# Polysketch attention and a channel block: key features, kv and numerators in 64-column tiles, key products on GpSimd, and a reordered first chunk

## The chip, the cores and the metric

The kernel runs on one core of one Trainium2 chip. The metric is the device time of one execution in microseconds, the median of several runs. The profile is of one execution; its span starts with the first profiled instruction and ends with the last, so it is some microseconds shorter than the time.

The engines are named as in the profile: PE is TensorE (PEld its weight loads), DVE is VectorE, ACT is ScalarE, POOL is GpSimd, SP is SyncE, which here only issues DMAs.

## The reference

Attention with a polynomial sketch in place of the softmax, and then a normalised channel block with a residual. There are 4 batches, 4 heads, 1088 tokens and a head width of 32; the sketch has r = 8, so a feature vector has 64 elements.

```python
def phi(x):                                   # S1, S2: 8 x 32
    a = np.einsum('rd,bhsd->bhsr', S1, x)
    b = np.einsum('rd,bhsd->bhsr', S2, x)
    return np.einsum('bhsi,bhsj->bhsij', a, b).reshape(*x.shape[:-1], 64)
q_p, k_p = phi(q), phi(k)
kv  = np.einsum('bhsf,bhsd->bhfd', k_p, v)
z   = np.sum(k_p, axis=2)
num = np.einsum('bhsf,bhfd->bhsd', q_p, kv)
den = np.einsum('bhsf,bhf->bhs', q_p, z)[..., None] + 1e-06
x   = (num / den) -> (4, 1088, 128)           # heads side by side
# channel block
xn  = (x - mean) / sqrt(var + 1e-06) * g_ln   # over the 128 channels
out = x + np.maximum(xn @ w_ch1, 0.0) @ w_ch2 # w_ch1 128 x 512, w_ch2 512 x 128
```

`S1`, `S2`, `g_ln`, `w_ch1` and `w_ch2` arrive as float64. [...]the kernel rounds them to float32 from their bit patterns.

## The kernel before

Everything is float32. The tokens are taken in 9 chunks: two chunks of 512 tokens for each batch (chunks 0 to 7), and the last 64 tokens of all four batches together as chunk 8. A float32 product of matrices is two passes in the profile, each with its weight load, so a line that issues one `matmul` shows two MATMUL records.

The pieces that the change touches. The features of the keys, in three parts of a batch (512, 512 and 64 tokens): a product into PSUM (`kf`), a copy to SBUF (`fs`), and the outer product of the two sketches (`kp`) on VectorE. The copy of v into a tile with a column of ones for each head is on GpSimd.

```python
def key_features(b, part):
    ...
    nc.gpsimd.tensor_copy(out=<v1, heads 33 apart>, in_=<vn>)
    kf = ps.tile([P, 512], F32, tag="xk", name="kf", bufs=1)      # shared with xp
    for i in range(tiles):
        nc.tensor.matmul(kf[0:m, 64*i : 64*i+64], kT[:, P*i : P*i+m], sk, ...)
    nc.scalar.copy(fs[0:m, 0:64*tiles], kf[0:m, 0:64*tiles])
    nc.vector.tensor_tensor(out=<kp>, in0=<fs, a repeated>, in1=<fs, b repeated>, op=ALU.mult)
```

The sum over the keys, `kv` and `z` in one product (33 columns a head). Two heads go in one product of 128 x 66, of which only the two diagonal blocks are used:

```python
def key_values(b):
    for t in range(NT):                       # 9 tiles of tokens
        for pair in range(2):
            nc.tensor.matmul(kvp[:, c], kp[0:m, <2 heads, 128 columns>], v1[0:m, <66 columns>], ...)
    for i in range(2):
        nc.vector.tensor_copy(out=<kvz, diagonal block>, in_=<kvp, diagonal block>)
```

The queries: `ab` holds both sketches repeated (64 rows, 128 columns), `qb` is a copy of one of them on ScalarE, `qp` their product on VectorE. The numerators `nd` (and denominators) are products with 128 tokens as columns; in the last chunk, where four batches share a tile, with 32:

```python
def numerators(c, i2):
    for i in range(2):
        for pair in range(2):
            if c < LAST:
                nc.tensor.matmul(nd[:, o:o+66], qp[:, <128 tokens>], kvzs[b][:, pc], ...)
            else:
                for b in range(B):
                    nc.tensor.matmul(nd[32*b : 32*b+32, o:o+66], qp[:, t:t+32], kvzs[b][:, pc], ...)
    den = nd + 1e-6; rden = 1/den; x = nd * rden     # VectorE
```

The channel block of a chunk: `x` is transposed (`xp`, then the copy `xT` on ScalarE), four products with the first weight (`hp`, then `hT` with the ReLU on ScalarE), sixteen with the second (`po`), and the sum `ob` on VectorE. Centring is folded into the first weight (`w1p`), and the inverse root of the variance is applied only in `ob`. The variance is `bn_stats` and `bn_aggr` on VectorE, a square root on ScalarE, and five small VectorE operations (`root`).

The order of work, which fixes the order in each engine's queue (`nb` is the next batch, in every even chunk):

```python
for c in range(LAST + 1):
    nb = ...
    if nb: key_rows(nb, 0); key_rows(nb, 1)
    hidden(c, 0); hidden(c, 1)
    query_features(c + 2, 0)
    hidden(c, 2)
    if nb: key_features(nb, 0)
    hidden(c, 3)
    numerators(c + 1, 0); numerators(c + 1, 1)
    if nb: key_rows(nb, 2); key_features(nb, 1)
    statistics(c + 1)
    second(c)
    if nb: key_features(nb, 2)
    root(c + 1)
    result(c)
    turn_x(c + 1)
    query_rows(c + 3)
    query_features(c + 2, 1)
    if nb: key_values(nb)
```

Ahead of the loop stand the rounding of the weights, the keys of batch 0, and the queries and numerators of chunk 0. The rounding of a weight is three bit operations on VectorE, five arithmetic operations on GpSimd, one more on VectorE and a last product on GpSimd.

Of the kernel before, what the change touches and what calls it, by code (L numbers as in the profile page):

```python
# [23 lines left out]
def kernel(  # L24
# [27 lines left out]

    nc = tc.nc
# [7 lines left out]
    NT = 9  # L61
# [11 lines left out]
    ps = ctx.enter_context(tc.tile_pool(name="ps", bufs=2, space=bass.MemoryType.PSUM))  # L73
    ctx.enter_context(tc.manual_schedule())

# [4 lines left out]
    s_raw = raw_tile([R2, D], S1, "s_raw")  # L80
    nc.scalar.dma_start(out=s_raw[0:R, :], in_=S1)
    nc.sync.dma_start(out=s_raw[R:R2, :], in_=S2)

    kn, qn, vn = {}, {}, {}

    def load_rows(store, src, tag, b):
        t = store[b] = consts.tile([P, G * D], F32, name=f"{tag}{b}")
        nc.sync.dma_start(
            out=t, in_=bass.AP(src.tensor, src.offset + b * H * S * D, [[G * D, P], [1, G * D]])
        )  # L90

    def load_v(b):
        base = v.offset + b * H * S * D
        vt = vn[b] = consts.tile([P, NT * DM], F32, name=f"vn{b}")
        for p0 in range(4):
            nc.sync.dma_start(
                out=_ap(vt, 32 * p0, 32, 0, [[8 * D, H], [1, 8 * D]]),
                in_=bass.AP(
                    v.tensor, base + 8 * p0 * D, [[G * D, 32], [S * D, H], [1, 8 * D]]
                ),  # L100
            )
        for r in range(2):
            nc.sync.dma_start(
                out=_ap(vt, 32 * r, 32, 8 * DM, [[D, H], [1, D]]),
                in_=bass.AP(
                    v.tensor, base + (32 + r) * D, [[G * D, 32], [S * D, H], [1, D]]
                ),
            )

    load_rows(kn, k, "kn", 0)  # L110
    load_rows(qn, q, "qn", 0)
    g_raw = raw_tile([P, 1], moe_g_ln, "g_raw")
    nc.scalar.dma_start(out=g_raw, in_=moe_g_ln.rearrange("(p o) -> p o", o=1))
    w1_raw = raw_tile([P, DH], moe_w_ch1, "w1_raw")
    nc.scalar.dma_start(out=w1_raw, in_=moe_w_ch1)
    w2_raw = raw_tile([P, JC * DM], moe_w_ch2, "w2_raw")
    nc.scalar.dma_start(
# [3 lines left out]
    load_v(0)  # L121
    for b in range(1, B):
        load_rows(kn, k, "kn", b)
        load_v(b)
        load_rows(qn, q, "qn", b)


    def rounded(dst, raw, eng):

        np_, n = dst.shape
        words = raw.bitcast(U32)
        lo, hi = words[:, 0 : 2 * n : 2], words[:, 1 : 2 * n : 2]

        def temp(tag, dtype):
            return work.tile([P, n], dtype, tag=f"{tag}{n}", name=tag)[0:np_, :]

        bits, ex, sign = (temp(tag, U32) for tag in ("bits", "ex", "sign"))
        mant = temp("mant", F32)  # L140
        bit, two = nc.vector.tensor_scalar, nc.vector.scalar_tensor_tensor
        ts = eng.tensor_scalar
        bit(out=ex, in0=hi, scalar1=20, scalar2=0x7FF,  # L143
            op0=ALU.logical_shift_right, op1=ALU.bitwise_and)
        bit(out=bits, in0=hi, scalar1=0xFFFFF, scalar2=None, op0=ALU.bitwise_and)
        bit(out=sign, in0=hi, scalar1=0x80000000, scalar2=None, op0=ALU.bitwise_and)  # L146
        yield
        ts(out=ex, in0=ex, scalar1=1023.0 - 127.0, scalar2=0.0, op0=ALU.subtract, op1=ALU.max)
        ts(out=ex, in0=ex, scalar1=255.0, scalar2=None, op0=ALU.min)
        ts(out=mant, in0=bits, scalar1=2.0**-20, scalar2=1.0, op0=ALU.mult, op1=ALU.add)  # L150
        low = temp("low", F32)
        ts(out=low, in0=lo, scalar1=2.0**-52, scalar2=None, op0=ALU.mult)
        eng.tensor_tensor(out=mant, in0=mant, in1=low, op=ALU.add)
        yield
        two(out=ex, in0=ex, scalar=23, in1=sign, op0=ALU.logical_shift_left, op1=ALU.bitwise_or)
        eng.tensor_tensor(out=dst, in0=mant, in1=ex.bitcast(F32), op=ALU.mult)

    def as_f32(raw, name, eng):

        if raw.dtype == F32:  # L160
            return raw, iter(())
        t = consts.tile(list(raw.shape), F32, name=name)
        return t, rounded(t, raw, eng)


    warm = small.tile([P, 1], F32, tag="warm", name="warm")
    nc.vector.memset(warm, 1.0)
# [10 lines left out]
    for h in range(H):  # L178
# [3 lines left out]
    center = consts.tile([P, P], F32, name="center")  # L182
    nc.gpsimd.tensor_scalar(
        out=center, in0=ident, scalar1=-1.0 / DM, scalar2=None, op0=ALU.add
    )

    kvzs = [consts.tile([P, 2 * 2 * D1], F32, name=f"kvz{b}") for b in range(B)]
    v1s = [consts.tile([P, NT * W], F32, name=f"v1_{i}") for i in range(2)]
    for t in v1s:
        nc.gpsimd.memset(_ap(t, 0, P, D, [[D1, 8 * H]]), 1.0)  # L190
        nc.gpsimd.memset(_ap(t, 0, 64, 8 * W + D, [[D1, H]]), 1.0)
    for t in kvzs:
        nc.gpsimd.memset(t, 0.0)
# [13 lines left out]
    sp = ps.tile([P, 512], F32, tag="nd", name="sp")  # L207
# [7 lines left out]


    def blocks(dst, src, half):

        nc.vector.transpose(  # L219
            _ap(dst, 0, P, 0, [[32, 4], [P, 4], [1, 32]]),  # L220
            _ap(src, 0, P, 4 * half * D, [[8 * D, 4], [D, 4], [1, D]]),
        )
# [11 lines left out]
    def key_features(b, part):  # L234
        t0, tiles, m = (4 * part, 4, P) if part < 2 else (8, 1, 64)
        if part == 0:
            kps[b] = work.tile([P, NT * H * F], F32, tag="kp", name="kp")
        v1, kT, kp = v1s[b % 2], kTs.pop((b, part)), kps[b]
        vj = 8 if part < 2 else 1
        nc.gpsimd.tensor_copy(  # L240
            out=_ap(v1, 0, m, t0 * W, [[W, tiles], [D1, H], [1, D]]),
            in_=_ap(vn[b], 0, m, t0 * D if part < 2 else 8 * DM, [[D, tiles], [vj * D, H], [1, D]]),
        )
        kf = ps.tile([P, 512], F32, tag="xk", name="kf", bufs=1)
        for i in range(tiles):
            nc.tensor.matmul(  # L246
                kf[0:m, 64 * i : 64 * i + 64], kT[:, P * i : P * i + m], sk,
                start=True, stop=True,
            )
        fs = work.tile([P, 4 * H * R2], F32, tag="fs", name="fs")  # L250
        nc.scalar.copy(fs[0:m, 0 : 64 * tiles], kf[0:m, 0 : 64 * tiles])  # L251
        nc.vector.tensor_tensor(  # L252
# [6 lines left out]
    def key_values(b):  # L259
        kvp = ps.tile([P, 512], F32, tag="nd", name="kvp")  # L260
        v1, kp, kvz = v1s[b % 2], kps.pop(b), kvzs[b]

        for t in range(NT):
            m = P if t < 8 else 64
            for pair in range(2):
                c = slice(2 * D1 * pair, 2 * D1 * (pair + 1))
                nc.tensor.matmul(  # L267
                    kvp[:, c],
                    kp[0:m, H * F * t + 2 * F * pair : H * F * t + 2 * F * (pair + 1)],
                    v1[0:m, W * t + c.start : W * t + c.stop],  # L270
                    start=(t == 0 and pair == 0), stop=(t == NT - 1), skip_group_check=True,
                )
        for i in range(2):
            nc.vector.tensor_copy(  # L274
                out=_ap(kvz, F * i, F, D1 * i, [[2 * D1, 2], [1, D1]]),
                in_=_ap(kvp, F * i, F, D1 * i, [[2 * D1, 2], [1, D1]]),
            )

    qTs, qps, xs, rs, mvs, xTs, hTs, pos = {}, {}, {}, {}, {}, {}, {}, {}
# [14 lines left out]
    def query_features(c, i2):  # L294


        if c > LAST or (c == LAST and i2):
            return
        qT = qTs[c]
        ab = ps.tile([P, 1024], F32, tag="ab", name="ab", bufs=1)  # L300
        for o, w in ((0, wb), (256, wa)):
            for pair in range(2):
                rows = slice(64 * pair, 64 * pair + 64)
                nc.tensor.matmul(  # L304
                    ab[:, 512 * pair + o : 512 * pair + o + 256],
                    w[rows, :], qT[rows, 256 * i2 : 256 * i2 + 256], start=True, stop=True,
                )
        qb = work.tile([P, 512], F32, tag="qb", name="qb")
        two = [[256, 2], [1, 256]]
        nc.scalar.copy(_ap(qb, 0, P, 0, two), _ap(ab, 0, P, 0, [[512, 2], [1, 256]]))  # L310
        p = qps[c, i2] = work.tile([P, 512], F32, tag="qp", name="qp", bufs=4)
        nc.vector.tensor_tensor(  # L312
            out=_ap(p, 0, P, 0, two), in0=_ap(ab, 0, P, 256, [[512, 2], [1, 256]]),
            in1=_ap(qb, 0, P, 0, two), op=ALU.mult,
        )

    def numerators(c, i2):

        if c > LAST or (c == LAST and i2):
            return  # L320
        if i2 == 0:
            xs[c] = work.tile([P, 512], F32, tag="x", name="x", bufs=3)
        qp, x = qps.pop((c, i2)), xs[c]
        nd = ps.tile([P, 512], F32, tag="nd", name="nd")
        for i in range(2):
            for pair in range(2):
                o = W * i + 2 * D1 * pair
                pc = slice(2 * D1 * pair, 2 * D1 * (pair + 1))
                if c < LAST:
                    nc.tensor.matmul(  # L330
                        nd[:, o : o + 2 * D1],
                        qp[:, 256 * pair + P * i : 256 * pair + P * i + P],
# [210 lines left out]
```

## Time and profile before

| What | Value |
|---|---|
| time, median of 3 runs | 172.49 us (171.52 to 173.51) |
| span of the profiled execution | 168.6 us |
| PE busy, instructions | 141.2 us, 893 |
| PEld busy | 109.5 us |
| DVE busy, instructions | 88.6 us, 291 |
| ACT busy, instructions | 43.1 us, 86 |
| POOL busy, instructions | 26.9 us, 50 |
| HBM read, written | 7.74 MB, 2.23 MB |

In the groups of a profile, "L267 PE MATMUL kvp<-v,kp" is the matmul of line 267 that writes the tile kvp from v and kp; behind it stand the shape of the array's tile (rows*columns), the shape of the output and the number of records, and then the busy time, the mean duration of one in ns, and the idle time of the engine just ahead of it with what ended it. A mean duration of a matmul includes its way through the array; what a pass costs in a stream is the length of the stretch over the number of passes, as the chain gives it.

### The profile page before, as it was taken

Reading aid. Unit: us, or ns where it says so; the run is one execution under the profiler, and the core shown is the slowest. Engines: PE = TensorE matmul, PEld = TensorE weight load, DVE = VectorE, ACT = ScalarE, POOL = GpSimd, SP = SyncE. Lnnn points to the kernel's source line nnn. Section 1 sums busy time; section 2 is a strip of 40 time slices with the busy share of each in tenths; the row PEclk is TensorE's granted clock in tenths of the full one; section 3 lists DMA queues with packets and bytes.
Section 4 is the critical chain, followed back from the end, with each engine's and each line's share of the span. In section 5 each row is a group of like instructions: output and inputs, shape, how many; then the busy total and the mean of one; then the engine's idle time right before and its main releaser. Section 6 shows DMA issues by size and latency. Waiting matters only on the chain.

```text
span 168.6 us, 2403 instructions
## 1 busy us (share of the span) xinstructions
PE 141.2 (84%) x893; PEld 109.5 (65%) x893; DVE 88.6 (53%) x291; ACT 43.1 (26%) x86; POOL 26.9 (16%) x50
## 2 busy tenths in 40 slices
PE   0542999569079999999999999999999999989870
PEld 0441898544047978595697949759895884965760
DVE  4466102734954872178587326858761584662610
ACT  3010101014213030604512142362123316225130
POOL 7006940499440003000000000000000000000000
PEclk9999999999858999999999999999999999999999
DMA  4897899300000002001100200020020002002021
GB/s 122 292 219 235 259 288 303 118 4 2 0 0 0 0 0 68 0 0 40 26 0 0 62 4 0 9 57 0 4 62 0 0 4 62 0 8 54 4 62 33
DMA packets 7196, 10.13 MB, mean 60 GB/s; under 512 B 2320, under 2 KB 5008, under 8 KB 7184
## 3 DMA queue, kind: packets, MB, share of 16 engines
q1 hardware_dynamic: 6352, 8.92, 19.6%
q10 hardware_dynamic: 832, 1.05, 2.2%
q8 instruction: 7, 0.11, 0.3%
q14 instruction: 5, 0.04, 0.1%
HBM read 7.74 MB, written 2.23 MB: 59 GB/s over the span
## 4 chain that ended last, share of the span: by engine, by line
PE 83%; DVE 8%; DMA 3%; ACT 2%; issue 1%; SPq 0%; DVEq 0%; ACTq 0%
PE hp L406 19%; PE po L416 18%; PE ab L304 13%; PE kvp L267 12%; PE nd L330 9%; PE kf L246 6%; PE xp L397 3%; DMA kn<-in_k_dram 3%; DVE qT L219 1%; ACT fs L251 1%; DVE r L385 1%; DVE sign L146 1%; PE w1p L474 1%; DVE kp L252 1%; DVE ex L143 1%
## 5 line engine op out<-in xcount | busy, mean ns | idle before, releaser
L406 PE MATMUL hp<-xT,w 128*128 128x512 f32 (+1 forms) x72 | 35.4, 611 | 1.2 <-ACT xT L399 1.2
L416 PE MATMUL po<-w_f,hT 128*128 128x128 f32 x272 | 32.4, 277 | 0.0
L416 PEld LDWEIGHTS po<-w_f,hT 128*128 128x128 f32 x272 | 31.2, 192 | 0.1
L409 ACT ACTIVATE hT<-hp 128x512 f32<-128x512 f32 (+1 forms) x36 | 20.5, 573 | 27.1 <-PE hp L406 27.0
L312 DVE TENSOR_TENSOR qp<-ab,qb 128x512 f32<-128x512 f32 x17 | 11.6, 684 | 26.3 <-ACT qb L310 26.2
L304 PE MATMUL ab<-qT,wb 64*128 64x256 f32 x68 | 14.4, 493 | 10.6 <-DVE qT L219 10.6
L267 PEld LDWEIGHTS kvp<-v,kp 128*128 128x128 f32 (+1 forms) x144 | 20.3, 226 | 2.0 <-issue 1.0
L267 PE MATMUL kvp<-v,kp 128*128 128x66 f32 (+1 forms) x144 | 21.3, 314 | 0.0
L406 PEld LDWEIGHTS hp<-xT,w 128*128 128x128 f32 x72 | 12.0, 193 | 13.4 <-issue 6.4
L330 PEld LDWEIGHTS nd<-kvz,qp 128*128 128x128 f32 x128 | 17.1, 209 | 4.0 <-issue 4.0
L310 ACT COPY qb<-ab 128x512 f32<-128x512 f32 x17 | 10.0, 585 | 33.2 <-PE ab L304 33.2
L304 PEld LDWEIGHTS ab<-qT,wb 64*128 64x128 f32 x68 | 6.3, 214 | 18.1 <-issue 12.7
L252 DVE TENSOR_TENSOR kp<-fs 128x1024 f32<-128x1024 f32 (+1 forms) x12 | 11.8, 984 | 11.0 <-ACT fs L251 11.0
L330 PE MATMUL nd<-kvz,qp 128*128 128x66 f32 x128 | 16.9, 291 | 0.0
L246 PEld LDWEIGHTS kf<-sk,kT 128*128 128x128 f32 (+1 forms) x72 | 11.1, 227 | 7.4 <-issue 5.1
L246 PE MATMUL kf<-sk,kT 128*128 128x64 f32 (+1 forms) x72 | 12.0, 314 | 4.6 <-DVE kT L232 3.0
L304 PE MATMUL ab<-qT,wa 64*128 64x256 f32 x68 | 12.5, 436 | 0.0
L429 DVE SCALAR_TENSOR_TENSOR ob<-po,rstd,x 128x128 f32<-128x128 f32 x34 | 9.6, 344 | 4.4 <-PE po L416 4.3
L240 POOL COPY v<-vn 128x512 f32<-128x512 f32 (+1 forms) x12 | 5.8, 518 | 27.5 <-issue 16.4
L274 DVE COPY kvz<-kvp 64x66 f32<-64x66 f32 x8 | 1.8, 224 | 14.4 <-PE kvp L267 14.4
L372 ACT ACTIVATE r<-va 128x4 f32<-128x4 f32 (+1 forms) x9 | 1.8, 205 | 29.3 <-DVE va L369 29.3
L365 DVE BATCH_NORM_STATS2 st<-x 128x6 f32<-128x128 f32 x34 | 9.1, 266 | 0.0
(67 smaller groups left out, 105.6 us busy)
## 6 DMA issues: line engine op xcount, KB each, us to landing
kn<-in_k_dram SPq DMA_DIRECT2D x4, 544.0 KB, 4.8
qn<-in_q_dram SPq DMA_DIRECT2D x4, 544.0 KB, 5.5
vn<-in_v_dram SPq DMA_DIRECT2D x16, 128.0 KB, 5.5
out_dram<-ob SPq DMA_DIRECT2D x32, 64.0 KB, 1.7
w_raw<-in_moe_w_ch_dram ACTq DMA_DIRECT2D x2, 512.0 KB, 10.9
vn<-in_v_dram SPq DMA_DIRECT2D x8, 16.0 KB, 5.0
out_dram<-ob SPq DMA_DIRECT2D x4, 32.0 KB, 1.6
s_raw<-in_S_dram ACTq DMA_DIRECT2D x1, 2.0 KB
```

Of the source, the lines that this page charges most:

```text
L246: nc.tensor.matmul(kf[0:m, 64 * i : 64 * i + 64], kT[:, P * i : P * i + m], sk, start=True, stop=True,)
L252: nc.vector.tensor_tensor(out=_ap(kp, 0, m, t0 * H * F, [[F, tiles * H], [R, R], [1, R]]), in0=_ap(fs, 0, m, 0, [[R2, tiles * H], [1, R], ...
L267: nc.tensor.matmul(kvp[:, c], kp[0:m, H * F * t + 2 * F * pair : H * F * t + 2 * F * (pair + 1)], v1[0:m, W * t + c.start : W * t + c.stop ...
L304: nc.tensor.matmul(ab[:, 512 * pair + o : 512 * pair + o + 256], w[rows, :], qT[rows, 256 * i2 : 256 * i2 + 256], start=True, stop=True,)
L310: nc.scalar.copy(_ap(qb, 0, P, 0, two), _ap(ab, 0, P, 0, [[512, 2], [1, 256]]))
L312: nc.vector.tensor_tensor(out=_ap(p, 0, P, 0, two), in0=_ap(ab, 0, P, 256, [[512, 2], [1, 256]]), in1=_ap(qb, 0, P, 0, two), op=ALU.mult,)
L330: nc.tensor.matmul(nd[:, o : o + 2 * D1], qp[:, 256 * pair + P * i : 256 * pair + P * i + P], kvzs[CHUNKS[c][0]][:, pc], start=True, stop= ...
L365: nc.vector.bn_stats(out=st[:, 6 * i : 6 * i + 6], in_=x[:, DM * i : DM * (i + 1)])
L406: nc.tensor.matmul(hp[:, 0:n], w1[:, P * j : P * (j + 1)], xTs[c][:, 0:n], start=True, stop=True)
L409: nc.scalar.activation(hTs[c][:, 512 * j : 512 * j + n], hp[:, 0:n], AF.Relu)
L416: nc.tensor.matmul(po[:, DM * i : DM * (i + 1)], hT[:, 512 * j + P * i : 512 * j + P * i + P], w2[:, DM * j : DM * (j + 1)], start=(j == 0 ...
L429: nc.vector.scalar_tensor_tensor(out=ob[:, t], in0=po[:, t], scalar=rstd[:, i : i + 1], in1=x[:, t], op0=ALU.mult, op1=ALU.add,)
```

## The change

What it does, part by part:

- **64-column tiles.** `kf`, `kvp` and `nd` are computed in two tiles of 64 columns of the array, which alternate: key features and numerators take 64 tokens in each, and `kvp` one head in each, so that the unused off-diagonal blocks are no longer computed. The number of matmuls doubles.
- **Key outer products on GpSimd.** All but two of the parts (the first and third of batch 0). In exchange, the copies of kvz go from VectorE to ScalarE, and the copies of v for batch 0 to ScalarE.
- **The variance.** `bn_aggr` and the small operations of VectorE are replaced by ten small operations a chunk on GpSimd, which combine the two halves that `bn_stats` gives.
- **PSUM by hand.** One tile covers all eight banks, and each use names its bank: 0 and 1 for nd and half of ab, 2 and 3 for kf, kvp and the other half of ab, 4 and 5 for hp, 6 for po, 7 for xp.
- **The order.** The four products of `hidden` stand together; then the numerators of the next chunk, the keys or kv of the next batch, and `second`. Keys come in odd chunks, kv in even ones; both features of the queries of chunk c + 2 come last, between `xp` and the next `hidden`.
- **The head.** The first loads are split and reordered (the first 512 columns of k first, w1 before v). In the rounding, three steps go to ScalarE (ReLU and copy with bias and scale), and two of GpSimd's into VectorE operations. The gains go into `center` and no longer into w1.
- **Tokens.** A chunk has other tokens than before (16 consecutive ones for each group instead of 4 from each run of 8); loads and stores follow.

The diff, cut to its core:

```diff
-    ps = ctx.enter_context(tc.tile_pool(name="ps", bufs=2, space=bass.MemoryType.PSUM))
+    banks = ps.tile([P, 8 * 512], F32, name="banks")
...
 # loads
+    load_rows(kn, k, 0, 0, 512)
+    load_rows(kn, k, 0, 512)
+    nc.sync.dma_start(out=w1_raw, in_=moe_w_ch1)
+    load_v(0, 0)
+    load_rows(qn, q, 0, 0, 512)
+    load_v(0, 1)
+    load_v(0, 2)
+    load_rows(qn, q, 0, 512)
+    nc.sync.dma_start(out=w2_raw..., in_=moe_w_ch2...)
...
 # rounding
+        act(over, ex, AF.Relu, bias=low_e[0:np_, :])
+        act(ex, over, AF.Relu, bias=top_e[0:np_, :], scale=-1.0)
+        act(mant, bits, AF.Copy, bias=1.0, scale=2.0**-20)
         yield
+        stt(out=ex, in0=ex, scalar=23, in1=sign, op0=ALU.logical_shift_left, op1=ALU.bitwise_xor)
+        stt(out=mant, in0=lo, scalar=2.0**-52, in1=mant, op0=ALU.mult, op1=ALU.add)
+        last.tensor_tensor(out=dst, in0=mant, in1=ex.bitcast(F32), op=ALU.mult)
...
-        out=center, in0=ident, scalar1=-1.0 / DM, scalar2=None, op0=ALU.add
+        out=center, in0=ident, scalar1=-1.0 / DM, scalar2=g_f, op0=ALU.add, op1=ALU.mult
...
 # key_features
+        kT, kp, kf = kTs.pop((b, part)), kps[b], bank(at)
         for i in range(tiles):
+            for u in range(0, m, 64):
+                nc.tensor.matmul(
+                    kf[u : u + 64, 64 * i : 64 * i + 64],
+                    kT[:, P * i + u : P * i + u + 64], sk, start=True, stop=True,
+                )
...
-        nc.vector.tensor_tensor(
+        eng.tensor_tensor(
             out=_ap(kp, ...), in0=_ap(fs, ...), in1=_ap(fs, ...), op=ALU.mult)
...
 # key_values
-            for pair in range(2):
+            for h in range(H):
                 nc.tensor.matmul(
+                    kvp[F * (h % 2) : F * (h % 2) + F, D1 * (h // 2) : D1 * (h // 2 + 1)],
+                    kp[0:m, H * F * t + F * h : H * F * t + F * (h + 1)],
+                    v1[0:m, W * t + D1 * h : W * t + D1 * (h + 1)], ...)
...
 # numerators
+        step = 64 if c < LAST else 32
...
+                    for u in range(0, P, step):
                         nc.tensor.matmul(
+                            nd[u : u + step, o : o + 2 * D1], qp[:, t : t + step],
+                            kvz[:, 2 * D1 * pair : 2 * D1 * (pair + 1)], start=True, stop=True,
                         )
...
 # statistics
-            nc.vector.bn_aggr(...)
+        tt(out=d, in0=of(1), in1=of(4), op=ALU.subtract)      # GpSimd
+        tt(out=s, in0=of(2), in1=of(5), op=ALU.add)
+        tt(out=d, in0=d, in1=d, op=ALU.mult)
+        ts(out=s, in0=s, scalar1=1.0 / DM, scalar2=1e-6, op0=ALU.mult, op1=ALU.add)
+        ts(out=d, in0=d, scalar1=0.25, scalar2=None, op0=ALU.mult)
+        tt(out=va, in0=d, in1=s, op=ALU.add)
+        nc.scalar.activation(r1, va, AF.Sqrt)
...
 # before the loop
+    key_features(0, 0, 4, nc.vector)
+    key_features(0, 1, 5, nc.gpsimd)
     next(w1_steps, None)
+    key_features(0, 2, 6, nc.vector)
...
+    key_tokens(0, 0, nc.scalar)    # and parts 1, 2
+    query_features(0)
     for _ in w1_steps:
         pass
+    key_values(0, 7)
+    numerators(0)
+    fill(1)
+    key_rows(1, 0)
+    key_features(1, 0, 2, nc.gpsimd)
+    ... w1p, turn_x(0), query_rows(1), query_features(1), first steps of w2, key_rows(1, 1), key_rows(1, 2)
...
     for c in range(LAST + 1):
+        b = c // 2 + 1
+        for j in range(JC):
+            hidden(c, j)
+        if c == 0:
+            for _ in w2_steps:
+                pass
+            key_features(1, 1, 2, nc.gpsimd)
+            key_features(1, 2, 3, nc.gpsimd)
+            for part in range(3):
+                key_tokens(1, part, nc.gpsimd)
+        numerators(c + 1)
+        if c % 2 == 0 and b < B:
+            key_values(b, 3)
+        if c % 2 == 1 and b + 1 < B:
+            fill(b + 1)
+            for part in range(3):
+                key_tokens(b + 1, part, nc.gpsimd)
+                key_rows(b + 1, part)
+                key_features(b + 1, part, 2 + part % 2, nc.gpsimd)
+        if c == 0:
+            statistics(0)
+            root(0)
         statistics(c + 1)
         second(c)
+        turn_x(c + 1)
+        query_rows(c + 2)
         root(c + 1)
         result(c)
+        query_features(c + 2)
```

## The prediction

> **What bounds the kernel now.** I read the table of stretches first, then the chain, then the timeline around what they point to. Busy shares over the whole span are no use here, because the span has three different parts. In the stretches (start:end, length, then PE, PEld, DVE, ACT and POOL busy with their instruction counts, granted clock, DMA share, GB/s):
>
> ```profile
> 0.00:47.49 47.49, 27.37 (x114) 21.66 (x114) 22.41 (x59) 7.13 (x14) 24.61 (x46) 0.98 0.58 164
> ...
> 66.53:96.90 30.37, 30.08 (x208) 23.45 (x207) 18.65 (x62) 9.65 (x19) 0.41 (x2) 1.00 0.08 19
> 96.90:127.26 30.36, 30.06 (x207) 23.45 (x207) 18.82 (x62) 9.65 (x19) 0.00 (x0) 1.00 0.08 19
> ```
>
> From 66.5 us on, two chunks of tokens take 30.36 us and TensorE is busy for 30.1 of them: only its own work counts there. In the first 47.5 us it is busy for 27.4 us with 114 passes, which are half a pair's. The chain says what the passes cost (start, us, what):
>
> ```profile
> 18.36 7.86 PE kvp L267 x35
> ...
> 28.24 3.62 PE nd L330 x16
> ...
> 62.23 4.30 PE kvp L267 x36
> 66.53 1.91 PE hp L406 x4
> ...
> 71.43 1.73 PE nd L330 x16
> 73.16 3.62 PE po L416 x32
> ...
> 154.17 0.61 PE nd L338 x32
> ```
>
> Three readings. A kvp pass takes 7.86/35 = 225 ns early and 4.30/36 = 119 ns late, an nd pass 226 and 108 ns: the array runs at half rate up to about 37 us, though the granted clock reads 0.98. Second, nd and kvp stream 66 columns per pass, po 128, and yet a pass costs 108, 119 and 3.62/32 = 113 ns: it is not the streaming that sets it, but the load of 128 columns of weights. Third, L338, the last chunk's numerators, runs in four tiles of 32 columns: 32 passes in 0.61 us, 19 ns each, 76 ns for a round of four. A 64-column load is in the trace too:
>
> ```profile
> 90.25 0.19 PEld L246 LDWEIGHTS kf<-sk,kT 128*64 128x64 f32 x2
> ```
>
> One such load lasts 132 ns at least (its group's minimum), two end after 190, so they start some 55 ns apart, half of the 107 that lie between 128-column ones.
>
> The head of the kernel is a chain over several engines. Two waits show it:
>
> ```profile
> 31.78 1.26 POOL L156 TENSOR_TENSOR w_f<-mant,ex 128x512 f32<-128x512 f32 x1 [8.77 <-DVE ex L155]
> ...
> 47.49 1.23 PE L304 MATMUL ab<-qT,wb 64*128 64x256 f32 x4 [5.14 <-DVE qT L219]
> ```
>
> The rounding of w1 to float32 ends at 33.0, its product with the gains at 35.0, and the second weight, the statistics and two transposes then hold VectorE until 47.35, with TensorE idle for 5.14 us.
>
> [...] here L153 takes 1268 ns for 128x512 on Pool and L252 takes 1225 ns for 128x1024 on VectorE, so 2.07 times. [...] the same r L385 lasts 1.11 us at 44.5, during Pool's w_f, and 0.16 at 91.6.
>
> **The change, TensorE in the steady part.** With two 64-column tiles side by side a round is the larger of a 64-column load (55) and a stream of 66 columns (55), with a little over: 58 ns for two passes.
> - nd: 32 passes a chunk instead of 16, 16 rounds x 58 = 0.93, [...] 1.0 us against 1.73. Saves 0.7 a chunk.
> - kvp: each head alone, 33 columns instead of 66 (the off-diagonal half is no longer computed): 72 passes, 36 rounds x 58 = 2.1 us against 4.30. Saves 2.2 a batch.
> - kf: 16 passes a part, 8 x 58 = 0.46 against 0.86, twice, and the third part unchanged: 1.2 against 2.0. Saves 0.8 a batch.
> - hp's four products now stand together: 3.6 us against 1.91 twice (8 streams of 0.427, one exposed load). po 3.63, xp 0.5, ab 2.1 stay.
> A chunk is then 3.6+3.63+0.5+2.1 = 9.8, [...] 10.0, with nd 11.0; with kf 12.2, with kvp 13.1. Two chunks: 25.3 against 30.36 if nothing else holds them.
>
> **Pool, off the path until it is on it.** The key products of batches 2 and 3 go to Pool: 1024 elements x 2.48 ns (L153) = 2.5 us, two a batch, and 0.7 for the third, between copies of 0.63. Behind them on Pool now stand the variance operations of the next chunk, six small dependent ones, which I put at 0.25 us each (a choice; no such chain is in this trace), and ScalarE's square root, which stands ahead of the copy xT in its queue. Times from the chunk's start: hp, nd and first kf done 5.2, fs copied 5.7, first product 8.2, copy 8.9, second 11.4, third 12.4, variance 13.9, square root 14.1, xT 14.7. TensorE would have wanted xT at 12.2. So in chunks 1 and 3 it waits 2.5 us: they take 14.75. In the other chunks the variance is done some 8.5 us in, ahead of the transposes at 9. VectorE loses the products, the aggregates (6.2 us in all) and four of five root operations; it had 12 us of 30 free already, so that gives nothing.
>
> **The head.** What I get by walking each queue of the new order with durations of the old trace, TensorE at half rate:
> - sk at 5.9 (was 5.5: the rounding of S now passes through ScalarE, behind its table load). The three kf parts have a bank each and run through: 6.65 to 8.8, instead of to 14.2.
> - keys on VectorE and Pool in parallel until 11.6; w1's bits by 11.5, ScalarE's three steps by 12.8, v copies 14.3; qT at 13.1, ab to 17.3.
> - kvp 36 x 115 ns = 4.1, to 21.5 (was 26.5); kvz on ScalarE, nd to 24.0 (was 31.9); x at 25.
> - w1 is ready at 21.4 and needs no product with the gains (they are in center: 1.86 us of Pool gone); kf of batch 1, w1p, xp, ab, and hp of chunk 0 starts at 32.5 (was 40.4).
> - ScalarE's three steps for w2 stand ahead of hT: hp stops for 2.3 and ends at 38.6. Then the new wait: kvp of batch 1 needs Pool's second product and copies, which end at 44.4; kvp to 45.3, po to 49, xp, ab: hp of chunk 1 starts at about 52. It was 66.5.
>
> **The sum.** 52 + 14.75 + 13.1 + 14.75 + 13.1 + 11.0 + 10.0 + 8.6 (chunks 1 to 7, the sixth with half an ab, the seventh with the small nd and the exposed transpose) = 137.3. From there to the end is 9.3 us as before (159.28 to 168.6). Span 146.6. The time is 172.49 at a span of 168.6, so 3.9 more: 150.5. I expect some of it to be lost to half-rate stretches after the idle times that I have in the head, and say 152.0.
>
> **Rivals.** (1) The tiles give nothing: two column tiles don't load at the same time, and a pass of 64 columns costs 55 alone. Then nd costs as much as before, kf as well, kvp 72 x 55 = 4.0. That takes 0.7 x 7 + 3 x 3 = about 14 away from the gain, but in chunks 1 and 3 Pool is then not waited for as long, and the time is 160 to 163. L338 speaks against it: four loads and four streams in 76 ns. (2) Pool becomes the bound: with its own access pattern (each factor repeated eight times) a key product costs 4 us instead of 2.5. Then chunks 1 and 3 and the head each lose 3 more, 161. For it: no such pattern is on Pool in this trace; against: a four-dimensional copy there takes 633 ns for 512, no worse than plain ones. (3) The head doesn't get shorter: loads land later (v in packets of half the size, more issues on one queue), and ScalarE has v copies, rounding and fs in one queue. Half of the head's 14 us gone would mean 159. The old head waited for DMA only for v until 14.3, and the new one wants v at 12.8. (4) The array leaves half rate earlier[...]: up to 4 us less, 148.
>
> **Range and chances.** Rivals 1 to 3 each cost 7 to 11 us alone; I give each about one in seven, and their combinations are slower than 163. The other side is 146. So 145 to 163. Slower than before would need all three. Faster by 2% means under 169: 0.93; within 2%: 0.05; slower: 0.02.
>
> **What would show it.** Right: nd in about 1.0 us a chunk, kvp in 2.1, chunks 5 and 6, which have no keys to compute, at 21 to 22 us together, hp waiting 2 to 3 us for xT in just two chunks, with Pool's variance behind it; hp of chunk 1 at 50 to 54 us. Wrong: nd at 1.7 (tiles in turn), a Pool product over 3 us, waits for xT in every chunk (small Pool operations dearer than 0.25), or a first ab later than 14 us.

## The result and the profile after

The changed kernel takes 150.61 us (median of 4) against 172.82 for the kernel before on the same chip: a ratio of **0.863 (0.856 to 0.870)**. The prediction said 152.0, in a range of 145 to 163. A second comparison gave 148.72 us and 0.864 (0.858 to 0.870). Some executions here are disturbed (151.9 to 155.1 us for the changed kernel at a granted clock of 0.93 to 0.94, the others 148.7 to 149.3 at 0.96): the ratios leave them out, the medians do not, and the profile shown below is that of the second, undisturbed run.

I cut both spans where a hidden stage (`hp`, now L431) starts. Chunk 0's work overlaps the loads, so everything up to `hp` of chunk 1 is called the head.

| us | before | after | predicted |
|---|---|---|---|
| head, to hp of chunk 1 | 66.5 | 50.45 | 52 |
| chunks 1 and 3 (keys) | 30.36 for a pair | 15.27, 15.89 | 14.75 each |
| chunks 2 and 4 (kv) | | 13.14, 13.14 | 13.1 each |
| chunks 5, 6, 7 | | 10.95, 10.08, 8.85 | 11.0, 10.0, 8.6 |
| rest | 9.3 | 8.9 | 9.3 |
| span | 168.6 | 146.7 | 146.6 |

The table of stretches after, with the columns as in the prediction (start:end, length, then PE, PEld, DVE, ACT, POOL busy, granted clock, DMA share, GB/s):

```profile
0.00:50.45 50.45, 31.44 (x376) 24.37 (x376) 23.13 (x65) 17.18 (x38) 17.61 (x54) 0.93 0.56 156
50.45:65.72 15.27, 12.50 (x128) 9.07 (x126) 6.05 (x19) 4.54 (x11) 6.51 (x12) 1.00 0.06 16
65.72:78.86 13.14, 13.13 (x164) 9.96 (x164) 6.18 (x22) 5.11 (x11) 3.19 (x15) 1.00 0.10 25
78.86:94.75 15.89, 14.00 (x128) 10.60 (x126) 6.63 (x21) 5.12 (x11) 6.91 (x15) 0.89 0.05 14
...
107.89:128.92 21.03, 21.03 (x178) 14.81 (x176) 10.97 (x39) 8.12 (x15) 3.81 (x20) 1.00 0.10 25
```

In the third and fifth line TensorE's busy time is the length of the stretch: nothing but its own work counts there. In the second it lacks 2.8 us, in the fourth 1.9, and the fourth also has 1.5 us more work than the second for the same passes. The head holds 19 us without a busy TensorE.

What the passes cost now, from the chain of waits (start, us, what):

```profile
17.73 2.74 PE banks L285 x72
...
65.72 3.80 PE banks L431 x8
69.52 1.09 PE banks L353 x32
70.61 2.19 PE banks L285 x72
72.80 3.77 PE banks L440 x32
76.57 0.44 PE banks L422 x4
77.01 1.93 PE banks L323 x16
```

L353 is nd, L285 kvp. The 32 passes of nd take 1.09 us, 34 ns each, where 16 took 1.73; the 72 of kvp take 2.19, 30 ns each, where 36 took 4.30. L440 is `po`, which is unchanged, at 3.77 for 32 passes: this is its full rate, to be remembered below.

Where TensorE is stopped, from its timeline (start, us, line, what; in brackets the idle time before and what ended it):

```profile
13.95 1.23 PE L323 MATMUL banks<-qT,wb 64*128 64x256 f32 x4 [4.78 <-DVE qT L233]
...
34.12 1.98 PE L431 MATMUL banks<-xT,w 128*128 128x512 f32 x4 [2.40 <-ACT hT L434]
...
40.41 2.63 PE L285 MATMUL banks<-v,kp 128*64 128x33 f32 x72 [2.64 <-POOL v L256]
42.97 5.19 PE L440 MATMUL banks<-w_f,hT 128*128 128x128 f32 x32
...
57.22 0.99 PE L265 MATMUL banks<-sk,kT 128*64 128x64 f32 x22 [1.88 <-DVE kT L233]
...
85.64 1.63 PE L265 MATMUL banks<-sk,kT 128*64 128x64 f32 x34 [1.89 <-DVE kT L233]
87.19 5.26 PE L440 MATMUL banks<-w_f,hT 128*128 128x128 f32 x32
```

Four things are to be seen. The wait for Pool's copies of v ahead of kvp of batch 1 is there, as predicted, with 2.64 us. In the key chunks (57.22, 85.64) the key features wait 1.9 us for the transposed keys, which the prediction doesn't have. `po` twice takes 5.2 instead of 3.8 us, both times a little after a stop. And the first queries still wait 4.78.

The order in VectorE's queue explains the wait for kT. From its timeline in chunk 1 and, for later, two records of the step that extracts a weight's exponent:

```profile
9.70 2.17 DVE L157 TENSOR_SCALAR ex<-w_raw 128x512 uint32<-128x512 uint32 x1
...
31.13 0.42 DVE L157 TENSOR_SCALAR ex<-w_raw 128x512 uint32<-128x512 uint32 x1
...
54.91 0.17 DVE L359 TENSOR_SCALAR den<-banks 128x8 f32<-128x8 f32 x1 [3.04 <-PE banks L353]
...
56.12 0.42 DVE L364 TENSOR_TENSOR x<-banks,rden 128x256 f32<-128x256 f32 x1
56.46 1.29 DVE L233 STREAM_TRANSPOSE kT<-kn 128x512 f32<-128x512 f32 x2
```

VectorE idles for 3.04 us, then works off den and x, and only then transposes the keys, because the program has `numerators(c + 1)` ahead of `key_rows`. TensorE has nothing else in the meantime. What Pool does in the same chunk:

```profile
58.40 1.95 POOL L271 TENSOR_TENSOR kp<-fs 128x1024 f32<-128x1024 f32 x1 [9.70 <-ACT fs L270]
60.29 0.61 POOL L256 COPY v<-vn 128x512 f32<-128x512 f32 x1
60.86 1.95 POOL L271 TENSOR_TENSOR kp<-fs 128x1024 f32<-128x1024 f32 x1
62.75 0.28 POOL L256 COPY v<-vn 64x128 f32<-64x128 f32 x1
63.00 0.62 POOL L271 TENSOR_TENSOR kp<-fs 64x256 f32<-64x256 f32 x1
...
64.76 0.20 POOL L395 TENSOR_TENSOR va<-d,s 128x4 f32<-128x4 f32 x1
```

The variance ends at 65.0, then come the square root and xT, and `hp` starts at 65.72, after a wait of 0.89. That is the wait of the prediction, at a third of its size.

### The profile page after: what moved, and what is told of

It reads as the page before. It is cut to its first block, busy times and chain, and to the rows that moved or that the text cites. A ratio compares the mean times of both kernels' runs of the same rounds, so it can differ in the third digit from the quotient of the medians.

```text
span 150.1 us, 3118 instructions
## 1 busy us (share of the span) xinstructions
PE 121.2 (81%) x1229; PEld 90.3 (60%) x1229; DVE 62.6 (42%) x194; ACT 49.7 (33%) x106; POOL 42.2 (28%) x136
## 4 chain that ended last, share of the span: by engine, by line
PE 61%; issue 14%; DVE 10%; POOL 6%; ACT 4%; DMA 2%; ACTq 0%; DVEq 0%; POOLq 0%
PE banks L440 17%; PE banks L431 17%; PE banks L323 9%; PE banks L285 6%; PE banks L353 4%; PE banks L265 3%; PE banks L422 2%; POOL kp L271 2%; DVE ex L157 2%; DVE x L364 2%; DMA s_raw<-in_S_dram 2%; PE banks L495 1%; POOL v L256 1%; DVE kT L233 1%; DVE kp L271 1%
## 5 line engine op out<-in xcount | busy, mean ns | idle before, releaser
L431 PE MATMUL banks<-xT,w 128*128 128x512 f32 (+1 forms) x72 | 34.1, 613 | 3.8 <-ACT hT L434 2.4
L440 PE MATMUL banks<-w_f,hT 128*128 128x128 f32 x272 | 36.2, 296 | 0.0
L440 PEld LDWEIGHTS banks<-w_f,hT 128*128 128x128 f32 x272 | 34.7, 210 | 0.6
L434 ACT ACTIVATE hT<-banks 128x512 f32<-128x512 f32 (+1 forms) x36 | 20.5, 573 | 12.4 <-PE banks L431 12.3
L431 PEld LDWEIGHTS banks<-xT,w 128*128 128x128 f32 x72 | 11.8, 192 | 21.3 <-ACT hT L434 12.4
L271 POOL TENSOR_TENSOR kp<-fs 128x1024 f32<-128x1024 f32 (+1 forms) x10 | 15.6, 1568 | 30.4 <-ACT fs L270 30.4
L332 DVE TENSOR_TENSOR qp<-banks,qb 128x512 f32<-128x512 f32 x17 | 11.5, 689 | 13.9 <-ACT qb L328 13.9
L323 PE MATMUL banks<-qT,wb 64*128 64x256 f32 x68 | 12.1, 436 | 4.8 <-DVE qT L233 4.8
L285 PE MATMUL banks<-v,kp 128*64 128x33 f32 (+1 forms) x288 | 11.3, 241 | 2.6 <-POOL v L256 2.6
L285 PEld LDWEIGHTS banks<-v,kp 128*64 128x64 f32 (+1 forms) x288 | 10.8, 159 | 3.3 <-POOL v L256 2.8
L353 PEld LDWEIGHTS banks<-kvz,qp 128*64 128x64 f32 (+1 forms) x288 | 8.7, 134 | 6.0 <-issue 5.3
L353 PE MATMUL banks<-kvz,qp 128*64 128x66 f32 (+1 forms) x288 | 10.0, 224 | 0.6 <-ACT kvz L292 0.6
```

What stands on the lines that cost most here:

```text
L271: eng.tensor_tensor(out=_ap(kp, 0, m, t0 * H * F, [[F, tiles * H], [R, R], [1, R]]), in0=_ap(fs, 0, m, 0, [[R2, tiles * H], [1, R], [0, R] ...
L285: nc.tensor.matmul(kvp[F * (h % 2) : F * (h % 2) + F, D1 * (h // 2) : D1 * (h // 2 + 1)], kp[0:m, H * F * t + F * h : H * F * t + F * (h + ...
L323: nc.tensor.matmul(bank(2 * i2 + pair)[:, o : o + 256], w[rows, :], qT[rows, 256 * i2 : 256 * i2 + 256], start=True, stop=True,)
L332: nc.vector.tensor_tensor(out=_ap(p, 0, P, 0, two), in0=_ap(banks, 0, P, 1024 * i2 + 256, [[512, 2], [1, 256]]), in1=_ap(qb, 0, P, 0, two) ...
L353: nc.tensor.matmul(nd[u : u + step, o : o + 2 * D1], qp[:, t : t + step], kvz[:, 2 * D1 * pair : 2 * D1 * (pair + 1)], start=True, stop=True,)
L431: nc.tensor.matmul(hp[:, 0:n], w1[:, P * j : P * (j + 1)], xTs[c][:, 0:n], start=True, stop=True)
```

## Experiments

The theory at this point: the tiles bring most of the gain; the reordering brings the rest in the head and costs something in the key chunks; what is left is three waits (kT behind x, v behind Pool's products, hT behind w2's rounding) and half-rate stretches that follow them. Times are medians; ratios are to the kernel before on the same chip (172.0 to 172.4 us in the three groups of runs). The rest of the change was not taken apart further: the variance on Pool, the PSUM banks and the other tokens were not tried alone.

**The same kernel again.**

> The changed kernel once more, unaltered, on the chip of the three experiments beside it, for a second profile. Every theory expects 148 to 152 us. The question is whether the head repeats: in the first profile the array runs at half rate from 41 to 50 us (kvp of batch 1 in 4.2 us, po of chunk 0 in 6.4). If that is fixed by the program, it is there again; if [...] those stretches differ from run to run by up to 5 us while chunks 2 and 4 to 8 repeat within 0.1 us.

148.72 us (148.44 to 149.01), 0.864. Its profile is the one above. The first profile of the same kernel differs from it mainly where the array was at half rate: there kvp of batch 1 takes 4.20 us and `po` of chunk 0 6.42 (here 2.65 and 5.19), the head ends at 54.10, and the slow `po` of the key chunks is that of chunk 1 (4.62). Chunks 2 and 4 to 8 agree within 0.1 us. So these stretches are not fixed by the program.

**The change without its tiles, and the tiles without the rest.** In the first, kf, kvp and nd of the changed kernel go back to 128 columns; in the second, only these three get tiles in the kernel before.

```diff
-            for u in range(0, m, 64):
-                nc.tensor.matmul(kf[u : u + 64, ...], kT[:, P * i + u : ... + 64], sk, ...)
+            nc.tensor.matmul(kf[0:m, ...], kT[:, P * i : P * i + m], sk, ...)
-            for h in range(H):
+            for pair in range(2):              # kvp, and the diagonal blocks of kvz
-        step = 64 if c < LAST else 32
+        step = P if c < LAST else 32           # nd
```

> The changed kernel with 128-column products for key features, kv and numerators (kv again with its unused off-diagonal blocks), all else kept. Theory A, the weight load of 128 columns sets the cost of a pass and two 64-column tiles halve it: nd 1.09 to 1.73 us in seven chunks (4.5 us), kvp 2.19 to 4.3 three times in the loop or just ahead of it (6.3), kf 1.4 to 2.0 twice (1.2), and about 4 in the head: 16 us more, 164 to 167. Theory B, the gain is the new order and the head, and the tiles lie beside other waits: 3 to 6 us more, 153 to 156.

> The kernel before with the three products in 64-column tiles and nothing else of the change. Theory A: a pair of chunks takes 30.36 less 2 x 0.64 (nd), 2.1 (kvp) and 0.7 (kf), so 26.3, three and a half times, and some 5 us off the half-rate head: 172.5 less 18, 154 to 157. Theory B: the loop of the kernel before becomes bound by the waits behind its shorter products and the head stays as it is: 165 to 168.

Without tiles the ratio is 0.984 (0.979 to 0.989), about 2.7 us gained. It rests on four of 16 executions (168.25 to 168.59 us); the others took 172.5 to 178.3, and the median of all, 173.28 us, is no gain at all. That is slower than even theory A had it. The tiles alone give 154.34 us and 0.896 (0.887 to 0.904), 18 us gained. Together they gain 23.4 (0.1357 x 172.1), by the ratios 2.7 more than the sum. The stretches of the kernel with tiles alone, two chunks each:

```profile
58.01:84.90 26.89, 26.59 (x295) 18.98 (x291) 18.36 (x62) 9.65 (x19) 0.70 (x2) 1.00 0.09 21
84.90:111.79 26.89, 26.59 (x294) 18.98 (x291) 18.47 (x62) 9.65 (x19) 0.00 (x0) 1.00 0.09 21
```

A pair takes 26.89 instead of 30.36 us, while the changed kernel needs 15.27 + 13.14 = 28.4 for it. So from hp of chunk 1 to hp of chunk 8 the *old* order with tiles takes 84.9 us and the changed kernel 87.3. What the change has beside the tiles earns its keep in the head alone: 50.45 against 58.01.

**The key products back on VectorE.** The products of batches 0 to 3 run on VectorE; in the odd chunks the key features of parts 0 and 1 stand together, and the third key part comes after `second`, ahead of `turn_x` (these lines are left out below).

```diff
-    key_features(1, 0, 2, nc.gpsimd)
+    key_features(1, 0, 2, nc.vector)            # likewise all others
```

> The changed kernel with all key outer products on VectorE (for batches 2 and 3 the third part after the second product of weights, so that TensorE needn't wait for it). Theory A, VectorE had time to spare and Pool's place in the chain costs about as much as it frees: the wait of hp for xT in chunks 1 and 3 goes (about 1 us each), the wait of kf for kT stays, and the head ends within 2 us of where it does: 147 to 151, the same. Rival, the move to Pool is what makes the rest possible: nine products of 1.23 us come back to VectorE's queue ahead of the statistics, and the time is over 155.

146.33 us, 0.851 (0.844 to 0.858): the move to Pool costs 2.4 us rather than gaining anything. Head 47.40, because Pool's v copies no longer stand behind its products; chunk 1 takes 17.0, with `po` at half rate (5.46 us), so its gain of 3 us is partly lost again. In chunks 1 and 3 kf still waits 1.9 us for kT, and now the queries' product waits another 0.78 and 1.31 us for VectorE. The exponent step of w1 is short here. From the groups of this kernel (minimum, median, maximum in ns):

```profile
L157 DVE TENSOR_SCALAR ex<-w_raw x2: 418/420/421, 11.3 to 30.9; 128x512 uint32<-128x512 uint32 x2
```

In the changed kernel the same instruction takes 2169 ns at 9.70, while Pool multiplies from 9.5 on, and 419 at 31.1, when Pool is idle. So it takes 1.7 us longer while Pool multiplies; what holds it there, these runs do not show.

**One wait at a time.** Three cures, each alone: two parts of the keys transposed ahead of the numerators; the v copies of batch 1 ahead of Pool's second and third product; the second weight's three ScalarE steps ahead of the first hidden stage.

```diff
+        if c % 2 == 1 and b + 1 < B:            # keys early
+            key_rows(b + 1, 0); key_rows(b + 1, 1)
         numerators(c + 1)
...
     key_features(1, 0, 2, nc.gpsimd)
+    for part in range(3):                       # v copies early (were after the third product)
+        key_tokens(1, part, nc.gpsimd)
...
+    query_rows(1); next(w2_steps, None); next(w2_steps, None)    # w2 early (were after turn_x(0))
     w1p = bank(4)
```

> In chunks 1 and 3 the transposes of the next keys stand ahead of the numerators in VectorE's queue, so that kf needn't wait for them (1.88 us each in the second profile of the changed kernel). Theory A, these waits lengthen the odd chunks, first directly and then through the half-rate product of weights that follows them (5.2 us instead of 3.7 in chunk 3): chunks 1 and 3 fall from 15.3 and 15.9 to about 13.3, where Pool's queue (two products of 1.95, copies, variance) lets xT go, and the time from 148.7 to 144.5. Rival, the step of the prediction, that Pool's queue alone sets the odd chunks: its work starts with kf, so an earlier kf without a shorter queue leaves hp waiting for xT by 2 us or more, and the time falls by less than 2 us.

> The copies of v for batch 1 go to Pool's idle time ahead of the second weight, instead of behind the key products. Theory A, kvp of batch 1 waits for these copies alone (2.64 us): it starts at 38 instead of 40.4, then follows Pool's last product at 39.8, and everything after is some 2 to 3 us earlier: 145.5 to 147. Rival, the products are as late as the copies: under 0.7 us.

> ScalarE's three steps of rounding w2 go ahead of the copies of w1 and qb, instead of ahead of hT. Theory A, the stop of hp in chunk 0 (2.40 us, for hT) was put there by them: it vanishes, hp of chunk 0 ends at about 32.5 instead of 36, and Pool's products of batch 1 follow: 2 to 4 us less, 145 to 147. Rival, the next wait in the head (w2 on Pool, keys of batch 1) takes its place: under 1 us.

- Keys early: 145.29 us, 0.843 (0.836 to 0.849). Chunks 1 and 3 take 13.2 instead of 15.27 and 15.89, and `po` is never slow in them; 0.58 of waiting for the third part of the keys and 0.36 for xT are left.
- v early: 145.67 us, 0.848 (0.843 to 0.852). The wait ahead of kvp falls from 2.64 to 0.23, and the head to 47.63.
- w2 early: 147.32 us, 0.856 (0.851 to 0.862). The hidden stage of chunk 0 runs through in 3.8 us, and 2.4 us should have come of it, but hp of chunk 1 starts only 0.6 earlier (0.4 of the rest is a first `ab` that started later in this run). The timeline of this kernel shows where most went:

```profile
38.24 3.25 PE L285 MATMUL banks<-v,kp 128*64 128x33 f32 x72 [2.62 <-POOL v L256]
41.42 6.13 PE L440 MATMUL banks<-w_f,hT 128*128 128x128 f32 x32
```

The wait for v is as long as before, and `kvp` and `po` behind it take 3.25 and 6.13 us, where 2.63 and 5.19 stood and 2.4 and 3.8 are possible. A wait here thus costs twice: itself (2.62 us), and the rate behind it.

**Work that only fills idle time.** Identity products whose results nobody reads: first 9 and 11 of them in the head (ahead of the transpose of the sketch, and ahead of the first queries' product), then, in another kernel, 11 in the wait for v and 8 in each wait for kT.

```diff
+            for _ in range(11):
+                nc.tensor.matmul(bank(7)[:, 0:P], ident, ident, start=True, stop=True)
             key_values(b, 3)
```

> Twenty products of the identity with itself, into a bank that is overwritten later, fill TensorE's idle time in the head: nine ahead of the sketch's transpose, eleven between the key features and ab of chunk 0. They add work and nothing waits for them. Theory A, the array runs at half rate because it was idle, whatever the granted clock says: kf of batch 0 goes from 1.14 to 0.5 to 0.7 us, ab of chunk 0 from 3.8 to 2.1, and the time falls by 1.5 to 2.5 us. Rival, the first passes are slow for another reason (first use of the operands): nothing changes, or the fillers themselves delay ab, 148 to 150.

> The changed kernel with identity products in the two waits alone: 11 ahead of kvp of batch 1 (the wait for v of 2.6 us), 8 ahead of kf in chunks 1 and 3 (the wait for kT of 1.9 us). They end no wait. Theory A, an array that stands idle for about 2 us goes to half rate for the next stage: kvp of batch 1 takes 2.3 instead of 2.65 us, po of chunk 0 3.7 instead of 5.2, po of chunks 1 and 3 3.7 each, the waits for kT and v stay, xT of chunk 3 is waited for again (0.9), time 146 to 147.5. Rival B, half rate comes with the low share of busy work and not with the idle time: po stays at 5.2 in chunks 0 and 3 and the time at 148.5 to 149.

In the head: 148.14 us (144.65 to 151.67). One execution took 144.65 us and the other five 147.5 to 151.7, so a gain is neither shown nor excluded. Its profile does show that the first `ab` takes 1.93 instead of 3.79 us and `hp` of chunk 0 starts 2.75 earlier; but the waits for hT (2.40) and v (2.39) are still there, `kvp` of batch 1 now takes 4.11 us, and `hp` of chunk 1 starts at 50.55, as before. In the waits themselves: 147.19 us, 0.860 (0.856 to 0.864). Its timeline:

```profile
38.98 2.72 PE L521 MATMUL banks<-ident 128*128 128x128 f32 x22
41.63 2.41 PE L285 MATMUL banks<-v,kp 128*64 128x33 f32 x72
43.97 3.84 PE L440 MATMUL banks<-w_f,hT 128*128 128x128 f32 x32
...
65.43 3.80 PE L431 MATMUL banks<-xT,w 128*128 128x512 f32 x8 [0.91 <-ACT xT L424]
```

Nothing waits for less here, the filler stands where TensorE stood idle, and yet `kvp` and `po` are back at full rate. Chunk 3 takes 15.32 instead of 15.89, because `po` is fast and xT is waited for again. For the stop in the head this shows that idle time sets the rate of what follows, and the other profiles agree: with this stop unfilled (2.1 to 2.6 us; the two profiles of the changed kernel, keys early, w2 early, filler in the head) `po` of chunk 0 takes 5.2 to 6.4 us each time, and in the six profiles where it is filled, short or gone, 3.8. Chunk 3 alone would not show it: behind the unfilled waits of 1.9 us for kT `po` was slow (4.6 to 5.4 us) in 5 of 12 cases.

Stops of 1.9 to 2.6 us were enough for half rate here, but not each time: after the stop in chunk 1 (1.88 us) `po` stayed fast, 3.84 us in the timeline, after an equal one in chunk 3 (1.89 us) it didn't, 5.26. What makes the difference, no run here shows. Nor does being busy always end half rate: in the kernel before, `ab`, `kvp`, `ab` and `nd` follow each other without a stop from 16.28 to 31.86 us, and nd, the last of them, still costs 226 ns a pass. Why is open.

**All cures together.** The three above, with a third buffer for kT (so that all three parts of the keys can go ahead of the numerators), and with the v copies of batches 2 and 3 moved out of the key chunks, one chunk earlier. Then the same with the head's filler (its 9 and 11 products stand where they stood before, not where the expectation puts them), and the same with the products on VectorE.

> The three separate cures together: keys of the next batch copied ahead of the numerators (that one alone measured 145.3 us against 148.7 of the changed kernel), v copies ahead of Pool's products in the head and two chunks earlier in the steady part (alone 145.7), the three steps of w2 ahead of the first hidden stage (alone 147.3). Theory A, the three waits are separate: the gains of 3.4, 3.0 and 1.4 us add up, head about 44.5 us, chunks 1 and 3 at 13.2 or below (no wait for kT, wait for xT below 0.3), time 141 to 142. Rival B, a next wait stands behind each: Pool's queue ends no earlier in the head, hidden of chunk 1 starts at 46 to 47 again and time is 144 to 145.

> The same and 9 identity products ahead of the first queries' product and 11 ahead of the first hidden stage, with results that nobody reads. Theory A, the idle time ahead of a stage sets the half rate of the array: the first ab takes 1.9 instead of 3.8 us and kvp of batch 1 and po of chunk 0 stay at 2.3 and 3.7, time 139 to 140. Rival B, the fillers only move the half-rate stretch to another place, as with the fillers alone (148.1 us against 148.7): time as without fillers, within 0.5 us.

> The kernel with the three cures, and the key products back on VectorE. Theory A, Pool's products still cost time there through its queue [...] (alone this gave 2.4 us): xT is never waited for in chunks 1 and 3, the head loses another 1 us as the exponent step of w2 is short again, time 1 to 2 us below the kernel with the three cures. Rival B, the cures have taken Pool off the path, and VectorE's longer queue (3.7 us of products a batch) delays the transposed keys or the sum of the hidden stage instead: same time or up to 1 us more.

| | us | ratio to before | head | chunks 1, 3 |
|---|---|---|---|---|
| changed kernel | 148.72 | 0.864 (0.858 to 0.870) | 50.45 | 15.27, 15.89 |
| all cures | 135.80 | 0.793 (0.789 to 0.797) | 43.72 | 12.40, 12.40 |
| with filler | 133.13 | 0.776 (0.771 to 0.781) | 41.42 | 12.39, 12.40 |
| with products on VectorE | 134.95 | 0.789 (0.785 to 0.793) | 44.34 | 12.21, 12.22 |

Alone, the cures gained 3.4, 3.0 and 1.4 us, 7.9 in all; together they gain 12.9, more than either expectation. The stretches of the kernel with all cures say where:

```profile
0.00:43.72 43.72, 29.24 (x376) 22.21 (x376) 22.83 (x65) 17.22 (x38) 18.28 (x55) 0.96 0.62 179
43.72:56.12 12.40, 12.28 (x129) 8.92 (x127) 6.02 (x19) 4.64 (x11) 6.16 (x12) 1.00 0.08 20
...
69.26:81.66 12.40, 12.28 (x128) 8.92 (x127) 5.92 (x18) 4.61 (x11) 5.74 (x10) 1.00 0.07 18
```

In the head 6.7 us are gone: 2.4 of the stop for hT, 2.0 of the wait for v, and the rest mainly because `po` runs in 3.77 instead of 5.19. The key chunks lose 2.9 and 3.5 us, some 0.8 each more than with the keys early alone, which is what the third buffer and the emptier Pool queue add: TensorE is busy for 12.28 of 12.40 us. So some 1.6 of the 5.0 us above the sum come from these two additions, which no single cure had. The rest fits what w2 early showed: with one stop left, the gain elsewhere was partly taken back behind it (1.6 us in kvp and `po` there); with the stops for hT and v gone, it stays. The filler in the head, undecided alone, gains 2.7 us here, by its first `ab`, which starts 0.58 earlier and takes 2.00 us instead of 3.72:

```profile
13.29 2.00 PE banks L325 x16
```

Here the expectation of a gain of about 2 us held; its times did not, as they were set against a slower kernel, and kvp and `po` of chunk 0 ran at full rate without the filler. With the products on VectorE the result is 0.9 us below that on Pool at overlapping intervals: once Pool is off the path, it hardly matters where the products are. The version with filler beats both kernels, by 22% and by 10%.

## Why the prediction was right, and where it was not

- **Steady part: right.** nd 1.09 us for 1.0, kvp 2.19 for 2.1, hp 3.73 for 3.6; kf took 1.27 where nothing was waited for (all cures, products on VectorE) for 1.2. Chunks 2, 4, 5 and 6 came out within 0.1 us. The estimate of a round, 58 ns for two passes, was a little low: nd takes 68, 1.09 us for its 16 rounds. It rests on the 55 ns between two 64-column loads and, for a stream of 66 columns, on 66/512 of the 0.43 us between two loads of hp (67.00 and 67.43 us in the profile before). What was put on top, from 0.93 to 1.0 us for nd and 0.2 for a chunk, was a choice of mine that rests on no trace.
- **Rival 1 (tiles in turn): refuted**, by the 34 ns of an nd pass, and by the kernel with tiles alone.
- **Chunks 1 and 3: right in size by luck, wrong in mechanism.** The step "hp waits 2.5 us for xT behind Pool's queue" was the one that failed. The Pool product takes 1.95 us, not 2.5: I took the 2.48 ns an element of a plain product of 512. (On the same product VectorE takes 1.22 us, so Pool is 1.6 times slower, not 2.07 as the two different shapes had it.) xT was therefore waited for 0.89 us in chunk 1 and not at all in chunk 3. In its place stand 1.9 us for kT, because I did not follow VectorE's queue where `key_rows` stands behind the numerators, and in chunk 3 another 1.5 of half rate. The runs with the keys early show it: the wait for kT, not Pool, was worth the 2 to 2.7 us a chunk.
- **Pool's small operations:** 0.25 us each was a fair choice; the six of the variance take 1.4 us in all, from 63.6 to 65.0.
- **The head: right within 1.6 us (2.1 in the first profile), by errors that offset each other.** The first ab started at 13.95, not 13.1, since the exponent step of w1 takes 2.17 us beside Pool's product, and 0.42 in the kernel with the products on VectorE; I had a like case before me (r L385, 1.11 us beside Pool's w_f and 0.16 later) and did not apply it. On the other side `kvp` of batch 0 took 2.74, not 4.1, and `hp` of chunk 0 started at 29.7, not 32.5: the array left half rate sooner (rival 4). The stop for hT was 2.40 for 2.3, and the wait for v came, with Pool's copies at 40.4 and not 44.4. `po` behind it at 5.19 us took 1.5 back.
- **Rivals 2 and 3:** neither came. A key product took 1.95 us on Pool, not 4. Pool's products cost 2.4 us as long as the waits were there and less than these runs resolve once the waits were cured, and the head lost 16 us.
- **The sum:** the parts add to 146.6 and the span is 146.7, with the head 1.6 below and the key chunks 1.7 above: that they cancel is luck. Two terms on top were too large. The 3.9 between span and time mixed a profiled run of 170.5 us with a median of 172.49; the true difference is 1.9 there and 1.7 here. And the 1.5 that I added for half rate were not needed: such stretches came (1.4 us each in `po` of chunks 0 and 3), but the head had been walked at half rate where it no longer ran so.

## What to carry to other kernels

When column tiles make a stage that is bound by weight loads shorter (nd here from 1.73 to 1.09 us), every queue that fed it in time has to be walked again, VectorE's as well as that of the engine that got new work. Waits of some 2 us on TensorE can come with a second bill, since the stage after them may run slower (here `po` behind waits of 1.9 to 2.6 us took up to 6.4 us instead of 3.8): cure them together, and judge a cure by the stretch it is in, not by the end of the program. An engine with idle time is a fit place for work only if nothing in its queue stands between a short result and TensorE.

## Of the hardware, not expected

- Pool's product with both factors repeated by stride is cheaper for each element than the plain one: 1.95 us for 128x1024 (1.9 ns each) against 1.27 for 128x512 (2.5 ns). Part of that is size: 64x256 of the repeated product takes 0.62 us, 2.4 ns each.
- The granted clock tells only in part where half rate was. In the kernel before it reads 1.00 from 18.36 to 26.20 us, where a kvp pass takes 225 ns, twice its later time. In the first profile of the changed kernel it does follow: 0.50 over the kvp of 4.20 us (41.26 to 45.40), 0.56 over the `po` of 6.42 (45.40 to 51.70) and 0.81 over that of 4.62 (62.80 to 67.40).
